# Splitting one matmul of sixteen: the frequency-0 set of a Fourier stage on TensorE

## The chip, the cores and the metric

The kernel runs on one core of a Trainium2 chip. Its time is the device time of one execution, in microseconds (us). Of the kernel before there are three runs: 596.06, 594.47 and 595.36 us, median 595.36. The profile is of one further execution, which took 595.34 us; the instructions that it records span 593.6 us.

## The reference

The output mixes two branches of the same 2048 x 512 input by a gate per row:

```python
x = A_u
g = _sigmoid((x * gate_w).sum(-1, keepdims=True))
a = _A_ref(x, ...)      # a long convolution per channel
b = _B_ref(x, ...)      # h = (x W) * (x V);  b = h W2
return g * a + (1 - g) * b

# inside _A_ref
K = 2.0 * jnp.einsum("dn,dnl->dl", C, P).real     # a filter of 2048 taps per channel
Kf = jnp.fft.rfft(K, L2)                          # L2 = 4096
Uf = jnp.fft.rfft(u_t, L2)
y = jnp.fft.irfft(Uf * Kf[None, :, :], L2)[:, :, :L]
return y + u * D_skip[None, None, :]
```

All of it is in float32.

## The kernel before

**The two branches share TensorE.** The gated product (b) is made of large matmuls, 128 rows by 128 columns with 512 columns of data, in `product` and `down`; each float32 operand there is split in a high and a low part, and three products are added (tiles `xs`, `whi`, `wlo`, `pg`, `pu`, then `hh`, `hl`, `dhi`, `dlo`, `y`). These run from the first to the last microseconds. The convolution (a) is laid between them in pieces.

**The convolution.** The filter is computed in 16 blocks of 32 channels (`k_block`, a dense run of 64 small matmuls each). After every fourth block, `transforms(q)` handles one quarter q of the channels (128 of them). A transform of length 4096 is done in two stages of small matmuls. The first stage is done ahead and its results lie in memory (`su_d` for the input, `sk_d` for the filter). For each of T = 0 to 3, `m_load` fetches the parts (512 KB each for input and filter), `m_second` does the second stage, and `m_product` multiplies input and filter spectra on VectorE. After T = 1 and T = 3, `m_inverse` and later `m_last` go back and add to the output.

**A set of the second stage.** `m_second` fills four PSUM banks. The 128 x 128 array of TensorE is used as 16 squares of 32 x 32. The row group r (32 lanes of the input tile) and the column group c pick a square, `tile_position=(32 * r, 32 * c)`; square (r, c) reads lanes 32r to 32r+31 and writes partitions 32c to 32c+31 of bank r. Each matmul has 512 columns: 256 for the filter and the input of one half p, 256 for the other half. For all frequencies but one family both halves use the same matrix, `w.t[lanes, c]`. The family with frequency 0 lies at T = 0, r = 0, c = 0, since the entries of `w2` for k = 0 stand there; it needs another matrix for the second half, which lies at index 4 of `w`. For T = 0, `w2s` thus has five matrices instead of four; in the lanes of r = 1 to 3 its fifth is equal to its first.

Before the change, all four matmuls with c = 0 of a T = 0 set are cut in two. There are four such sets, one for each q.

**Eviction.** After a set, `evict` copies each bank to the tile `ev`, on ScalarE, and for the last q every second bank on VectorE. The tiles of PSUM are called `k` in the trace.

**Order.** All operations are entered as tasks with an estimated length (1.05 us for a set), and `Work.run` lays them out by those lengths; each engine then issues in that order. An operation waits for other engines through semaphores.

Of the kernel before, what the change touches and what calls it, by code (L numbers as in the profile page):

```python
# [18 lines left out]
P = 128  # L19
# [150 lines left out]
class Work:  # L170
# [27 lines left out]
    def add(self, engine, us, fn, r=(), w=(), rank=1, after=0.0, dma=0, hold=(), rows=(), many=0):  # L198


        task = Task(len(self.tasks), engine, us, fn, rank, after, dma)
        task.rows, task.many = rows, many
        self.tasks.append(task)
        clash = lambda p, q: p is None or q is None or p == q
        split = lambda x: x if isinstance(x, tuple) else (x, None)
        for tile, part in map(split, r):
            task.deps.update(t for p, t in tile.writers if clash(p, part))
        for tile, part in map(split, w):
            task.deps.update(t for p, t in tile.writers + tile.readers if clash(p, part))
        for tile, part in map(split, r):  # L210
            tile.readers.append((part, task))
        for tile, part in map(split, w):
            tile.writers.append((part, task))
        for tile, _ in map(split, [*r, *w, *hold]):
            if tile.pool and tile not in task.tiles:
                task.tiles.append(tile)
                tile.users.append(task)
        task.deps.discard(task)
        return task
# [105 lines left out]
def gated_mix_kernel(  # L325
# [16 lines left out]
    pe, dve, act, sp, pool_q = (InOrder(tc, e) for e in (nc.tensor, nc.vector, nc.scalar, nc.sync, nc.gpsimd))  # L342
# [22 lines left out]
    def new(pool, tag, shape, dtype=F32, bufs=1, loose=False):  # L365
        return work.tile(pools[pool], tag, shape, dtype, bufs, loose)

    def bank():
        return new("ps_k", "k", [P, D], bufs=4, loose=True)
# [603 lines left out]
    def x_table(b):  # L973

        x, ri, (su, di) = xtab[b], ris[b], sus[b]
        ps = new("tab", "ps", [P, TB, 4])
        lead = [(x, ("l", k)) for k in range(3)]
        tt(0.26, lambda: ps.t, lambda: x.t[:, 0, :, 0:4], lambda: x.t[:, 1, :, 0:4], ALU.add, lead, [ps])
        outer(
            x, lambda: x.t[:, :, :, 0:4], lambda: ps.t, lambda: ri.t[:, :, :, W_M],  # L980
            lambda: su.t[:, :, W_M], lambda: di.t[:, :, 4:11], [*lead, ps, ri, su, di],
        )
        return x
# [54 lines left out]
    def apart_of(q):  # L1038
        return work.LESS if q >= KT - 2 else work.APART
# [76 lines left out]
    def evict(q, n, us, to, src, r, w):  # L1116

        if q == KT - 1 and n % 2:
            add("dve", us + 0.1, lambda: dve.tensor_copy(to(), src()), r=r, w=w)
        else:  # L1120
            add("act", us, lambda: act.copy(to(), src()), r=r, w=w)
# [35 lines left out]
    def m_second(q, T, ins, w):  # L1157

        banks = [bank() for _ in range(4)]
        to = new("mid", "ev", [P, 2, 2, 2, 2 * P], bufs=2)  # L1160
        at, parts = ins

        def fn():
            src = at().rearrange("l (p c) w d -> l c p (w d)", p=2)
            for c in range(4):
                for r in range(4):
                    lanes, to = slice(32 * r, 32 * r + 32), banks[r].t[32 * c : 32 * c + 32]
                    pieces = [(c, to, src[lanes, c])]
                    if T == 0 and c == 0:

                        pieces = [(4 * p, to[:, 2 * P * p : 2 * P * p + 2 * P], src[lanes, c, p]) for p in range(2)]
                    for m, to, x in pieces:
                        pe.matmul(to, w.t[lanes, m], x, start=True, stop=True, tile_position=(32 * r, 32 * c))

        add("pe", 1.05, fn, r=[*parts, w], w=banks, rank=1, hold=[to], many=apart_of(q))
        for r in range(4):
            h, e = divmod(r, 2)
            evict(
                q, r, 0.59, lambda h=h, e=e: to.t[:, :, e, :, P * h : P * h + P],
                lambda r=r: banks[r].t.rearrange("l (p w d) -> l w p d", p=2, w=2), [banks[r]], [(to, r)],  # L1180
            )
        return to
# [198 lines left out]
    x = x_table(0)  # L1381
    for b in range(NB):
# [5 lines left out]
        if b + 1 < NB:  # L1388
            direct_powers(b + 1)
            leads(b + 1)  # L1390
            x = x_table(b + 1)
# [59 lines left out]
```

## Time and profile before

| | |
|---|---|
| median of three runs | 595.36 us (594.47 to 596.06) |
| profiled execution | 595.34 us, span 593.6 us |
| TensorE matmul busy | 579.7 us, 98% of the span |
| VectorE busy | 512.1 us, 86% |
| ScalarE busy | 401.8 us, 68% |
| granted TensorE clock, mean | 0.996 |

PE is the matmul side of TensorE, PEld its weight loads, DVE is VectorE, ACT ScalarE, POOL GpSimd, SP SyncE. L124 is the line through which the kernel issues all its operations, so rows are told apart by their tiles: `k<-in,w2s` and `k<-x,w2s` are matmuls of the second stage when their form is `32*32` (32 rows by 32 columns). In the rows of the trace, "start us, us" come first, and `x40` counts records. A float32 matmul of this type leaves two records, one for each of its two passes.

In the table of stretches a row gives the stretch, its length, busy time with the number of records, the granted clock, the DMA share and GB/s. In the table of waits a row ends with the us in total, the times and the longest.

### The profile page before, as it was taken

The numbers are of one execution on the slowest core, as the hardware profiler recorded it, in microseconds if no ns is written. First come the engines' busy times: TensorE is split into PE (matmuls) and PEld (weight loads), VectorE is DVE, ScalarE is ACT, GpSimd is POOL, SyncE is SP. The second block draws the span as 40 slices with busy tenths as digits, with TensorE's granted clock in tenths as the row PEclk, the third lists the DMA queues.
The fourth block names the chain that finished last, engine by engine and source line by source line (L and its number), as shares of the span: only waits on it lengthen the run. The fifth ranks groups of instructions, "written<-read, shape, count | busy, mean of one in ns | idle before, by whom it ended". The sixth has DMA issues, their size and how long they took to land.

```text
span 593.6 us, 14891 instructions
## 1 busy us (share of the span) xinstructions
PE 579.7 (98%) x6020; PEld 436.6 (74%) x6020; DVE 512.1 (86%) x812; ACT 401.8 (68%) x891; POOL 113.7 (19%) x159
## 2 busy tenths in 40 slices
PE   8899999999999999899999999999999899999996
PEld 5677676788877777687676877867877776777764
DVE  6998999999998999899999999996999972556845
ACT  5348898898679488878887675799786343433351
POOL 0003212411111231310123201112422104202011
PEclk9989999999999999999999999999999999999999
DMA  8998779896867697998789856899969349898887
GB/s 270 408 368 299 273 274 347 199 309 197 204 178 204 203 239 189 227 267 263 153 200 264 188 149 190 177 279 260 225 137 251 68 131 252 271 285 207 262 187 132
DMA packets 71687, 136.28 MB, mean 230 GB/s; under 512 B 6852, under 2 KB 35780, under 8 KB 69188
## 3 DMA queue, kind: packets, MB, share of 16 engines
q1 hardware_dynamic: 47668, 87.10, 43.0%
q0 software_dynamic: 23392, 47.98, 38.6%
q8 instruction: 47, 0.77, 0.5%
q10 hardware_dynamic: 560, 0.26, 0.2%
q14 instruction: 20, 0.16, 0.1%
HBM read 80.27 MB, written 55.05 MB: 228 GB/s over the span
## 4 chain that ended last, share of the span: by engine, by line
PE 90%; DVE 5%; issue 2%; ACT 2%; DMA 1%; DVEq 0%; SPq 0%; ACTq 0%
PE pg L124 25%; PE y L124 24%; PE pu L124 24%; PE k L124 16%; DVE x L124 1%; DMA y<-in_xT 1%; DVE v L124 1%; DVE wlo L124 1%; DVE in L124 0%; ACT acc L124 0%; DMA raw<-in_xT 0%; DVE h L124 0%; DVE dlo L124 0%; ACT L124 0%; ACT xs L124 0%
## 5 line engine op out<-in xcount | busy, mean ns | idle before, releaser
L124 PE MATMUL pg<-xs,whi 128*128 128x512 f32 x448 | 139.0, 391 | 0.5 <-ACT whi L124 0.5
L124 PE MATMUL pu<-xs,whi 128*128 128x512 f32 x448 | 138.6, 391 | 0.0
L124 PEld LDWEIGHTS pg<-xs,whi 128*128 128x128 f32 x448 | 84.4, 188 | 20.9 <-ACT whi L124 2.1
L124 PEld LDWEIGHTS pu<-xs,whi 128*128 128x128 f32 x448 | 84.4, 188 | 17.0
L124 PE MATMUL y<-dhi,hl 128*128 128x512 f32 x224 | 89.7, 400 | 4.3 <-ACT acc L124 2.2
L124 PE MATMUL pg<-xs,wlo 128*128 128x512 f32 x224 | 89.8, 401 | 2.2 <-issue 1.6
L124 PE MATMUL pu<-xs,wlo 128*128 128x512 f32 x224 | 90.3, 403 | 0.0
L124 PE MATMUL y<-dlo,hh 128*128 128x512 f32 x224 | 87.7, 391 | 0.2 <-DVE dlo L124 0.2
L124 PE MATMUL y<-dhi,hh 128*128 128x512 f32 x224 | 87.5, 391 | 0.0
L124 ACT COPY ev<-k 128x512 f32<-128x512 f32 x112 | 59.4, 599 | 22.6 <-PE k L124 22.5
L124 POOL DMA_DIRECT2D out<-acc x44 | 39.4, 972 | 154.9 <-ACT acc L124 150.3
L124 ACT CAST hh<-h 128x512 fp32r<-128x512 f32 x56 | 34.9, 623 | 45.7 <-DVE h L124 45.0
L124 PEld LDWEIGHTS y<-dhi,hl 128*128 128x128 f32 x224 | 42.0, 188 | 26.8 <-issue 10.6
L124 ACT ACTIVATE acc<-y,ngate 128x512 f32<-128x512 f32 x62 | 42.2, 690 | 27.5 <-PE y L124 24.4
L124 PEld LDWEIGHTS pu<-xs,wlo 128*128 128x128 f32 x224 | 42.1, 188 | 20.9 <-issue 10.5
L124 DVE TENSOR_TENSOR h<-pu,h 128x512 f32<-128x512 f32 x56 | 38.6, 690 | 21.6 <-PE pu L124 19.9
L124 PEld LDWEIGHTS pg<-xs,wlo 128*128 128x128 f32 x224 | 42.3, 189 | 17.0 <-issue 6.2
L124 ACT COPY h<-pg 128x512 f32<-128x512 f32 x56 | 33.0, 590 | 24.6 <-PE pg L124 18.2
L124 PEld LDWEIGHTS y<-dhi,hh 128*128 128x128 f32 x224 | 42.2, 188 | 9.1
L124 PEld LDWEIGHTS y<-dlo,hh 128*128 128x128 f32 x224 | 42.1, 188 | 8.6 <-DVE dlo L124 0.5
L124 DVE TENSOR_TENSOR hl<-h,hh 128x512 fp32r<-128x512 f32 x56 | 38.4, 686 | 4.0 <-ACT hh L124 3.9
L124 POOL DMA_DIRECT2D su_d<-ev x32 | 17.9, 577 | 94.4 <-ACT ev L124 94.4
(130 smaller groups left out, 985.4 us busy)
## 6 DMA issues: line engine op xcount, KB each, us to landing
xs<-xs_d SPq DMA_DIRECT2D x36, 512.0 KB, 6.1
out<-acc POOLq DMA_DIRECT2D x44, 256.0 KB, 5.4
raw<-in_wts SPq DMA_DIRECT2D x33, 256.0 KB, 6.1
xs_d<-xs SPq DMA_DIRECT2D x16, 512.0 KB, 6.0
su_d<-ev POOLq DMA_DIRECT2D x32, 256.0 KB, 6.7
y_d<-ts SPq DMA_DIRECT2D x28, 256.0 KB, 6.0
in<-su_d POOLq DMA_DIRECT2D x12, 512.0 KB, 7.7
sk_d<-ev SPq DMA_DIRECT2D x6, 1024.0 KB, 5.7
```

The lines of the kernel that those rows point to most:

```text
L124: got = getattr(self.engine, name)(*args, **kw)
```

## The change

For T = 0 only the matmul at r = 0, c = 0 is split. Its first half is issued first in the set, its second half last, with the 15 whole matmuls between. The other sets are issued as before, by the same loop over a list of jobs.

```diff
         def fn():
             src = at().rearrange("l (p c) w d -> l c p (w d)", p=2)
-            for c in range(4):
-                for r in range(4):
-                    lanes, to = slice(32 * r, 32 * r + 32), banks[r].t[32 * c : 32 * c + 32]
-                    pieces = [(c, to, src[lanes, c])]
-                    if T == 0 and c == 0:
-
-                        pieces = [(4 * p, to[:, 2 * P * p : 2 * P * p + 2 * P], src[lanes, c, p]) for p in range(2)]
-                    for m, to, x in pieces:
-                        pe.matmul(to, w.t[lanes, m], x, start=True, stop=True, tile_position=(32 * r, 32 * c))
+            jobs = [(r, c, c, slice(0, 2)) for c in range(4) for r in range(4)]
+            if T == 0:
+
+                jobs = [(0, 0, 0, 0), *jobs[1:], (0, 0, 4, 1)]
+            for r, c, m, p in jobs:
+                lanes = slice(32 * r, 32 * r + 32)
+                to = banks[r].t[32 * c : 32 * c + 32].rearrange("l (p d) -> l p d", p=2)[:, p]
+                pe.matmul(to, w.t[lanes, m], src[lanes, c, p], start=True, stop=True, tile_position=(32 * r, 32 * c))
```

On TensorE, the T = 0 set of the last quarter reads as follows (`k` a PSUM bank, `x` the loaded parts, `w2s` the matrices; minus before, plus after):

```order
 L124 MATMUL pu<-xs,wlo 128x512
 L124 MATMUL pu<-xs,whi 128x512 x2
-L124 MATMUL k<-x,w2s 32x256 x8
-L124 MATMUL k<-x,w2s 32x512 x12
+L124 MATMUL k<-x,w2s 32x256
+L124 MATMUL k<-x,w2s 32x512 x15
+L124 MATMUL k<-x,w2s 32x256
 L124 MATMUL pu<-xs,wlo 128x512
 L124 MATMUL pu<-xs,whi 128x512 x2
```

Eight halves and 12 whole matmuls became two halves and 15; what stands around the set did not move.

On ScalarE, the copies of the first T = 0 set out of PSUM (`ev<-k`), with the semaphores that each waits for:

```order
 L124 COPY h<-pg 128x512 [waits DVE_49,PE_49]
 L124 COPY ev<-k 128x2x2x128 [waits DMAHW3_49,PE_49]
-L124 COPY ev<-k 128x2x2x128 [waits PE_49] x3
+L124 COPY ev<-k 128x2x2x128 x3
 L124 CAST hh<-h 128x512 [waits DVE_49]
 L124 ACTIVATE v<-v 128x32x16 [waits DVE_49]
```

Bank 0 is now finished by the last matmul of the set, so the first copy waits for that one, and the three others have nothing left to wait for.

## Prediction

> **What bounds the kernel now.** I read the page first: busy shares, the slices, the chain that ended last. Then I asked the trace for the sets of the second Fourier stage, for what TensorE waits for, and for the places around its two late waits.
>
> ```profile
> PE 579.7 (98%) x6020; PEld 436.6 (74%) x6020; DVE 512.1 (86%) x812; ACT 401.8 (68%) x891; POOL 113.7 (19%) x159
> PEclk9989999999999999999999999999999999999999
> PE 90%; DVE 5%; issue 2%; ACT 2%; DMA 1%; DVEq 0%; SPq 0%; ACTq 0%
> 201.00:594.00 393.00, 384.49 (x4502) 1.00 0.82 211
> 588.46 0.39 PE L124 MATMUL y<-dhi,hh 128*128 128x512 f32 x1
> ```
>
> TensorE is busy for 98% of the span and holds 90% of the chain, at the full clock. The fourth row is TensorE alone from 201 us on, where the first changed set stands: 384.49 busy of 393.00, and about 5 of the missing 8.5 us lie behind its last matmul, the fifth row. So time taken from TensorE's own work should come off the end, unless TensorE then waits. Its waits from 201 us on are two:
>
> ```profile
> PE pg L124 <- issue: 1.6, 1, 1.6
> PE y L124 <- ACT acc L124: 1.5, 1, 1.5
> ```
>
> **What a split set costs today.** A set of the second stage is 16 matmuls of 32 rows by 32 columns, one for each square of the array, 512 columns wide. For T = 0 four of them are cut in two. The trace records each matmul of this type twice (two passes), so a plain set has 32 records and a T = 0 set 40. Two neighbours, with the matmul that follows each:
>
> ```profile
> 528.23 2.14 PE L124 MATMUL k<-x,w2s 32*32 32x256 f32 x40
> 530.30 0.50 PE L124 MATMUL pu<-xs,wlo 128*128 128x512 f32 x1
> 534.63 1.14 PE L124 MATMUL k<-x,w2s 32*32 32x512 f32 x32
> 535.70 0.50 PE L124 MATMUL y<-dhi,hl 128*128 128x512 f32 x1
> ```
>
> From the first matmul of the set to the next matmul behind it: 530.30 - 528.23 = 2.07 us for T = 0, 535.70 - 534.63 = 1.07 us for a plain one. The other three T = 0 sets and the plain ones read the same in a table of stretches (busy time, records):
>
> ```profile
> 201.40:203.50 2.10, 2.05 (x40) 1.00 0.81 314
> 209.85:210.93 1.08, 1.06 (x32) 1.00 1.01 307
> 316.10:318.18 2.08, 2.06 (x40) 1.00 1.23 205
> 432.93:435.00 2.07, 2.06 (x40) 1.00 0.04 8
> ```
>
> The four split sets thus pay 1.00 us each more than a plain set of equal arithmetic. Where that goes shows in the count of records begun by a given moment, first for the split set, then for the plain one (the matmul's duration in ns, first and last start, then the shapes):
>
> ```profile
> L124 PE MATMUL k<-x,w2s x12: 398/612/612, 528.2 to 528.3; 32*32 32x512 f32 x8, 32*32 32x256 f32 x4
> L124 PE MATMUL k<-x,w2s x16: 374/505/612, 528.2 to 528.5; 32*32 32x256 f32 x8, 32*32 32x512 f32 x8
> L124 PE MATMUL k<-x,w2s x18: 374/492/612, 528.2 to 528.7; 32*32 32x256 f32 x9, 32*32 32x512 f32 x9
> L124 PE MATMUL k<-x,w2s x33: 374/585/612, 528.2 to 528.9; 32*32 32x512 f32 x17, 32*32 32x256 f32 x16
> L124 PE MATMUL k<-x,w2s x40: 374/586/612, 528.2 to 529.8; 32*32 32x512 f32 x24, 32*32 32x256 f32 x16
> L124 PE MATMUL k<-x,w2s x16: 612/612/612, 534.6 to 534.7; 32*32 32x512 f32 x16
> ```
>
> In the plain set all 16 first passes begin within 0.1 us, one per square. In the split set only 12 do: four halves (their twins sit on the same squares and must wait) and eight full matmuls. That is 16 matmuls in hand, four of them held back. The seventeenth, the first of the last four full ones, begins only by 528.7, and the last record begins at 529.8 instead of about 0.55 us into the set. So my reading is that TensorE looks some 16 matmuls ahead, and that four twins in front stop the last column group.
>
> **The change, part by part.** Removed: three matmuls in each of four sets, 12 in all (24 records of matmul and 24 weight loads). Kept: one split pair, whose halves now stand first and last.
>
> The new set: the first half and 15 full matmuls are 16, so all squares begin at once as in the plain set. The second half is the seventeenth. In the old set the seventeenth began 0.4 to 0.5 us after the start (between the second and third row above). The four half passes of a square began between 528.2 and 528.9, so a half pass takes about 0.23 us, and the second half's two passes would run from 0.45 to 0.91 us of the set. The full squares run two passes of twice that, to 0.10 + 4 x 0.23 = 1.02 us. The second half is covered, by some 0.1 us. Set: 1.07 us.
>
> The unknown is that cover. Lower bound: a plain set's 1.07. Upper bound: the second half runs alone behind all others, two half passes and the rest of the drain, 1.07 + 0.53 = 1.60 us (0.53 is half a plain set, for half the columns). I take 1.07, nearest to the plain row. Sum: 4 x (2.07 - 1.07) = 4.0 us off TensorE.
>
> The page TensorE: Matmul & The Clock Gate of the Trainium skill says, in Part 3 (packing small matmuls), that a pack lasts one matmul plus about 4 ns for each further tile. By that, a sum from the number of matmuls would be 12 x 4 ns = 0.05 us. The 1.00 us that four further halves cost here does not agree with it, since twins share a square.
>
> Evictions: the four copies out of PSUM now all wait for the last matmul, because the second half ends bank 0. Before, the first copy went ahead:
>
> ```profile
> 316.12 2.13 PE L124 MATMUL k<-in,w2s 32*32 32x256 f32 x40
> 317.60 2.05 ACT L124 COPY ev<-k 128x512 f32<-128x512 f32 x4 [1.13 <-PE k L124]
> 319.18 0.69 DVE L124 TENSOR_TENSOR h<-pu,h 128x512 f32<-128x512 f32 x1 [1.18 <-PE pu L124]
> 322.04 0.70 DVE L124 TENSOR_TENSOR hl<-h,hh 128x512 fp32r<-128x512 f32 x1
> 323.10 0.39 PE L124 MATMUL y<-dhi,hl 128*128 128x512 f32 x1
> ```
>
> The copies began 1.48 us into that set (317.60 against the start at 316.12). They will begin at 1.14 (the plain set's length with its drain) plus a few hundredths, 0.3 us earlier in absolute time but 0.7 us later against TensorE. Behind them on ScalarE stands hh, and TensorE takes hl 0.36 us after it is made (323.10 - 322.74). VectorE was idle 1.18 us before h, so it can follow by 1.0 us; its row of work then sets hl, and hh (after copies that end near 319.4) is ready before that. Cost 0; with that cover gone, up to 0.3 us in a set.
>
> **The two waits.** The first changed set lies ahead of the wait at 244 us:
>
> ```profile
> 240.15 0.62 ACT L124 CAST whi<-raw 128x512 fp32r<-128x512 f32 x1 [2.17 <-PE y L124]
> 243.38 1.25 ACT L124 ACTIVATE acc<-y,ngate 128x512 f32<-128x512 f32 x2
> 244.10 0.50 PE L124 MATMUL y<-dhi,hl 128*128 128x512 f32 x1 [1.55 <-ACT acc L124]
> ```
>
> ScalarE is idle 2.17 us, then works without a pause until acc frees the accumulator. If that chain hangs on TensorE, as the row says, it moves with it. If it hangs on the arrival of raw, the first 1.0 us is lost. I count it as passed on.
>
> The second wait names no releaser. It follows a dense run of small matmuls, and only one packet moved in code ("instruction") just then:
>
> ```profile
> 459.85 2.07 PE L124 MATMUL k<-v,x 128*32 128x64 f32 x128
> 463.50 0.40 PE L124 MATMUL pg<-xs,wlo 128*128 128x512 f32 x1 [1.59 <-issue]
> q8 instruction: 47, 0.77, 0.5%
> q8 instruction: 1, 0.02, 5.1%
> ```
>
> The last row is the stretch from 461.0 to 462.2 us. I take it for late code: 47 packets of 16 KB carry TensorE's program, and the run eats 256 records in 2 us. The change makes the program shorter by 36 matmul and load records ahead of this place, so packets end elsewhere. The stall can go (-1.59) or stay (0). The three times of before, 594.47 to 596.06, differ by just that size, so the median holds it only in part; I take -0.6.
>
> **Sum.** Profiled execution: 595.34 us (span 593.6 and 1.7 around it), 0.02 from the median 595.36. 595.36 - 4.0 - 0.6 = 590.8 us.
>
> **Rivals.** (a) The chain at 244 us hangs on raw's transfer: one set's gain is lost, 591.8. For it: the 2.17 us of idle ScalarE; against it: the named releaser. 0.14. (b) The second half runs behind everything: 1.60 a set, 4 x 0.47 = 1.9 saved, 595.36 - 1.9 - 0.6 = 592.9. Against it, the seventeenth matmul of the old set begins while others run. 0.10. (c) T = 0 is slow for another reason than its twins, and a matmul less is worth only its issue: 16 start within 0.11 us, 12 x 0.007 = 0.1 us, 595.3. Against it, the stretch of late starts lies inside the set. That counts a pack as the Trainium skill's page TensorE: Matmul & The Clock Gate does, in Part 3. 0.06. (d) Slower: shifted packets starve TensorE behind more of its dense runs, 1.59 us each. From four new stalls on it is slower by over 0.3%: 595.36 - 4.0 + 4 x 1.59 = 597.7. Against it, one stall in 47 packets so far; 0.05.
>
> **The numbers.** The forecast has 0.65. A change under 0.3% (1.8 us, 593.6 to 597.1) can't be told from none. Faster: forecast, (a) and (b), 0.89, less a little for unknown waits, 0.87; same: (c) and that little, 0.08; slower 0.05. The range goes from the stall gone wholly with some luck of run to run (595.36 - 5.6 = 589.8, less 0.6) up past (b), 589.2 to 593.2; it leaves out (c), (d) and the tails.
>
> **What would show it.** Split sets of 34 records that last 1.07 us; 15 full first passes and one half within 0.1 us of their start; TensorE's wait at 243 us no longer than 1.6; the wait after the run near 460 us shorter or elsewhere. A set longer than 1.2 us breaks the reading of the 16 in hand; a wait at 243 us of 2.5 is (a).

## The result and the profile after

The changed kernel takes 591.47 us (median of nine, 588.79 to 593.89), the kernel before beside it 596.06 us (median of nine, 594.14 to 598.65). The medians lie 4.6 us apart. The ratio is 0.9921, with a 95% interval of 0.9895 to 0.9946, which is a gain of 3.2 to 6.3 us. Forecast was 595.36 to 590.8, also 4.6 us. Medians and ratios leave out one disturbed execution, of 1457.38 us, among the ten of the kernel with both edits below.

The profiled execution of the changed kernel took 588.79 us, with a span of 587.0. Its page (busy time of the engines, the granted clock in 40 slices, the chain that ended last) still shows a kernel that TensorE bounds:

```profile
PE 575.0 (98%) x5996; PEld 434.4 (74%) x5996; DVE 511.7 (87%) x812; ACT 401.3 (68%) x891; POOL 113.8 (19%) x159
PEclk9999999999999999999999999999999999999999
PE 89%; DVE 4%; DMA 2%; ACT 2%; issue 1%; DVEq 0%; SPq 0%; ACTq 0%
```

The busy time fell by 4.7 us (579.7 to 575.0), with 24 matmul records fewer (6020 to 5996). The timeline of TensorE shows a split set and the matmul behind it:

```profile
522.85 1.14 PE L124 MATMUL k<-x,w2s 32*32 32x256 f32 x34
523.92 0.50 PE L124 MATMUL pu<-xs,wlo 128*128 128x512 f32 x1
```

523.92 - 522.85 = 1.07 us, as in a plain set, and 1.00 less than before. The other three read 1.07 too. The records of this set begun by four moments (duration in ns, first and last start, shapes):

```profile
L124 PE MATMUL k<-x,w2s x16: 398/612/612, 522.8 to 522.9; 32*32 32x512 f32 x15, 32*32 32x256 f32 x1
L124 PE MATMUL k<-x,w2s x17: 374/612/612, 522.8 to 523.1; 32*32 32x512 f32 x15, 32*32 32x256 f32 x2
L124 PE MATMUL k<-x,w2s x33: 374/588/612, 522.8 to 523.4; 32*32 32x512 f32 x30, 32*32 32x256 f32 x3
L124 PE MATMUL k<-x,w2s x34: 374/588/612, 522.8 to 523.5; 32*32 32x512 f32 x30, 32*32 32x256 f32 x4
```

Fifteen whole matmuls and one half begin within 0.1 us. The half's second pass follows alone at 0.24 us, the second half's first pass among the second passes of the others, its last pass at 0.67 us. The last whole pass begins at 0.55 us and takes twice as long as a half pass, so it ends later: the second half is covered.

The evictions behind the second split set (timeline; in brackets the idle time ahead and what ended it):

```profile
313.56 2.06 ACT L124 COPY ev<-k 128x512 f32<-128x512 f32 x4 [0.99 <-PE k L124]
317.15 0.69 DVE L124 TENSOR_TENSOR hl<-h,hh 128x512 fp32r<-128x512 f32 x1
318.19 0.39 PE L124 MATMUL y<-dhi,hl 128*128 128x512 f32 x1
```

The copies begin 1.34 us after the set (313.56 against 312.22), 1.48 before. TensorE takes hl 0.35 us after it is made, 0.36 before: nothing lost.

TensorE's late waits are of the same two kinds, those without a releaser at other places (all its waits from 199.6 us on, then the timeline):

```profile
PE y L124 <- issue: 1.6, 1, 1.6
PE y L124 <- ACT acc L124: 0.3, 1, 0.3
PE k L124 <- issue: 0.2, 1, 0.2
```

```profile
240.11 0.50 PE L124 MATMUL y<-dhi,hl 128*128 128x512 f32 x1 [0.34 <-ACT acc L124]
413.21 0.39 PE L124 MATMUL y<-dlo,hh 128*128 128x512 f32 x1 [1.57 <-issue]
```

The wait for acc is 0.34 us in place of 1.55. The wait without a releaser, 1.59 us near 462 us before, stands at 411 us with 1.57 us. The third row is a small wait of the same kind, 0.25 us at 337.7 us; it took 0.11 us before, at 342.3 us.

Where the time between the two profiled executions goes, by the starts of the same matmuls:

| Matmul | before, us | after, us | ahead by |
|---|---|---|---|
| first split set | 201.45 | 199.68 | 1.77 |
| plain set behind it | 209.87 | 207.10 | 2.77 |
| matmul behind the wait for acc | 244.10 | 240.11 | 3.99 |
| second split set | 316.12 | 312.22 | 3.90 |
| matmul soon behind it | 324.55 | 319.64 | 4.91 |
| third split set (behind the new stall at 411) | 432.94 | 430.10 | 2.84 |
| plain set behind it | 447.67 | 443.82 | 3.85 |
| plain set behind the place of the old stall | 480.61 | 475.22 | 5.39 |
| fourth split set | 528.23 | 522.85 | 5.38 |
| plain set behind it | 534.63 | 528.22 | 6.41 |
| last matmul | 588.46 | 582.05 | 6.41 |

Each split set gives 1.00 us; a row of the table can hold up to 0.03 more from what lies between its two matmuls. The first 1.77 us lie ahead of all that was changed. Some 0.6 us are lost: 0.3 at the small wait near 340 us, 0.1 near 250 us, which no row explains, and 0.2 at the moved stall, around which the matmuls lose more than its idle time.

The lead at the first set is no gain of the change. TensorE in the first 60 us (busy, records, granted clock, DMA share, GB/s), the kernel before, the changed kernel, and a second profiled execution of the changed kernel:

```profile
0.00:60.00 60.00, 55.30 (x245) 0.97 0.94 337
```

```profile
0.00:60.00 60.00, 55.97 (x257) 1.00 0.96 349
```

```profile
0.00:60.00 60.00, 55.93 (x233) 0.97 0.90 328
```

With the clock at 0.97 the changed kernel's first split set began at 202.90 us, later than before. From the first split set to the last matmul, which leaves this out, the kernel before took 387.0 us and the changed kernel 382.4 us: 4.6 us. The second profiles of the two kernels give 388.1 and 383.4 us: 4.7 us.

### The profile page after: what moved, and what is told of

Same layout as the page of the kernel before. It is cut to its first block, busy times and chain, and to the rows that moved or that the text cites. A ratio compares the mean times of both kernels' runs of the same rounds, so it can differ in the third digit from the quotient of the medians.

```text
span 587.0 us, 14842 instructions
## 1 busy us (share of the span) xinstructions
PE 575.0 (98%) x5996; PEld 434.4 (74%) x5996; DVE 511.7 (87%) x812; ACT 401.3 (68%) x891; POOL 113.8 (19%) x159
## 4 chain that ended last, share of the span: by engine, by line
PE 89%; DVE 4%; DMA 2%; ACT 2%; issue 1%; DVEq 0%; SPq 0%; ACTq 0%
PE pg L124 25%; PE pu L124 24%; PE y L124 24%; PE k L124 16%; DMA raw<-in_wts 1%; DVE x L124 1%; DVE v L124 1%; DMA y<-in_xT 1%; ACT whi L124 0%; DVE in L124 0%; DMA raw<-in_xT 0%; ACT acc L124 0%; DVE h L124 0%; DVE dlo L124 0%; ACT L124 0%
```

## The experiments

Two theories on the sets stood against each other: TensorE holds 16 matmuls of this type in hand, and what a twin in hand takes is a place; or each matmul more costs something of its own. Two more questions were the wait near 462 us and the wait for acc. The diffs are against the changed kernel.

**All twins apart.** Four split squares as before the change, with the four first halves first and the four second halves last: 20 matmuls, as before.

```diff
-                jobs = [(0, 0, 0, 0), *jobs[1:], (0, 0, 4, 1)]
+                jobs = [(r, 0, 0, 0) for r in range(4)] + jobs[4:] + [(r, 0, 4, 1) for r in range(4)]
```

> All four halves pairs of the old kernel are kept (20 matmuls in a T = 0 set), but the four first halves stand first, the 12 whole matmuls next and the four second halves last. Theory, a look-ahead of 16 matmuls that frees a place only when the oldest matmul is done: all 16 squares begin at once, the four second halves enter from 0.43 us on and the last of them begins near 0.91 us, so the set lasts about 1.2 us, and the kernel takes 4 x 0.86 = 3.4 us less than the kernel before. Rival, the cost goes by the number of matmuls: 40 records, 2.07 us a set, no gain.

592.37 us against 594.26; ratio 0.9957 (0.993 to 0.9985), a gain of 0.9 to 4.2 us where 3.4 was expected. The timeline, and the records begun within 0.1 us:

```profile
527.44 1.29 PE L124 MATMUL k<-x,w2s 32*32 32x256 f32 x40
528.67 0.50 PE L124 MATMUL pu<-xs,wlo 128*128 128x512 f32 x1
```

```profile
L124 PE MATMUL k<-x,w2s x16: 398/612/612, 527.4 to 527.5; 32*32 32x512 f32 x12, 32*32 32x256 f32 x4
```

With all 20 matmuls the set takes 1.22 us. The order alone brings 0.84 of the 1.00 us. Sixteen squares start at once, and the last record begins at 0.92 us, where 0.91 was worked out from 16 in hand. The count of matmuls is not what made T = 0 slow.

**The pair in front.** As many matmuls as in the changed kernel, but the two halves next to each other at the head.

```diff
-                jobs = [(0, 0, 0, 0), *jobs[1:], (0, 0, 4, 1)]
+                jobs = [(0, 0, 0, 0), (0, 0, 4, 1), *jobs[1:]]
```

> Only the square with frequency 0 is split, as in the changed kernel, but its two halves stand one behind the other at the front. Theory: one place of 16 is held by the twin, the last whole matmul enters when the first half's first pass is done (0.43 us), its second pass begins at 0.86 us, and the set lasts 0.86 + 0.52 = 1.37 us. Rival, the order does not matter and the number of matmuls does: 1.07 us, as in the changed kernel.

592.98 us, in a single run. The timeline, and the records begun within 0.25 us of the start:

```profile
526.73 1.44 PE L124 MATMUL k<-x,w2s 32*32 32x256 f32 x34
528.10 0.50 PE L124 MATMUL pu<-xs,wlo 128*128 128x512 f32 x1
```

```profile
L124 PE MATMUL k<-x,w2s x16: 374/612/612, 526.7 to 527.0; 32*32 32x512 f32 x14, 32*32 32x256 f32 x2
```

1.37 us, 0.30 more than the changed kernel for the same 17 matmuls. Only 14 whole ones begin at once: the second half holds a place while its square is taken, and the fifteenth comes late.

**The pair at the end.**

```diff
-                jobs = [(0, 0, 0, 0), *jobs[1:], (0, 0, 4, 1)]
+                jobs = [*jobs[1:], (0, 0, 0, 0), (0, 0, 4, 1)]
```

> Only the square with frequency 0 is split, and both halves stand at the end. Theory (a place is freed by the oldest matmul alone): the second half's first pass enters when the first whole matmul's first pass is done, at 0.64 us, its second pass when that matmul's second pass is done, at 1.07 us, and the set lasts 1.07 + 0.30 = 1.37 us. Rival, a free square is all that a matmul waits for: the second half's passes begin at 0.55 and 0.77 us, inside the run of the others, and the set lasts 1.07 us.

591.34 us, in a single run. The timeline and the records begun by three moments:

```profile
525.15 1.44 PE L124 MATMUL k<-x,w2s 32*32 32x512 f32 x34
526.52 0.50 PE L124 MATMUL pu<-xs,wlo 128*128 128x512 f32 x1
```

```profile
L124 PE MATMUL k<-x,w2s x17: 373/612/612, 525.1 to 525.5; 32*32 32x512 f32 x15, 32*32 32x256 f32 x2
L124 PE MATMUL k<-x,w2s x33: 372/588/612, 525.1 to 525.8; 32*32 32x512 f32 x30, 32*32 32x256 f32 x3
L124 PE MATMUL k<-x,w2s x34: 372/588/612, 525.1 to 526.2; 32*32 32x512 f32 x30, 32*32 32x256 f32 x4
```

1.37 us again, by another way. All 16 squares start at once here; the second half is the seventeenth. Its square is free from 0.56 us (the first half's second pass starts at 0.34 and takes 0.22), but its first pass begins at 0.64 and its second only at 1.07 us. In the trace the passes of the oldest matmul start at 0.00 and 0.45 us, so they end near 0.45 and 0.88, and each pass of the second half begins 0.19 us behind one of them. So a place comes free when the oldest matmul is done, pass by pass, not when any is.

The first of the three rows shows something more. The first half is the last of the 16 in program order, yet its second pass is the only second pass begun by 525.5 (at 0.34 us; the whole ones' begin from 0.45). Matmuls on different squares thus do not start in strict program order. The Trainium skill's page TensorE: Matmul & The Clock Gate speaks in Part 3 of a reorder window 64 deep: a float32 matmul here is two loads and two passes, and 16 x 4 = 64 agrees with all three rows of starts. Its words that matmuls start strictly in order do not agree with this row.

**No split at all.**

```diff
-                jobs = [(0, 0, 0, 0), *jobs[1:], (0, 0, 4, 1)]
+                jobs = [*jobs]
```

> No matmul of the T = 0 set is split: 16 whole ones, so that the second half of frequency 0 uses the first half's matrix (the second matrix of that frequency is left out of the computation). Theory, the second half is covered in the changed kernel: 1.07 us a set, the same time as the changed kernel, within the runs' spread. Rival, the last half still costs something (each T = 0 set shorter than 1.07, or the kernel faster by more than 0.5 us beyond the changed one's gain of about 4.6 us): the cover was not whole.

589.17 us against 594.26; ratio 0.9894 (0.9831 to 0.9956), not to be told from the changed kernel's. The kernel leaves out the second matrix of frequency 0. The timeline:

```profile
524.46 1.14 PE L124 MATMUL k<-x,w2s 32*32 32x512 f32 x32
525.53 0.50 PE L124 MATMUL pu<-xs,wlo 128*128 128x512 f32 x1
```

1.07 us, as in the changed kernel: the second half, first and last as the change has it, adds nothing to the set. The medians alone can't decide, since 5.1 us against the changed kernel's 4.6 lies at the rival's mark of 0.5 us. In the traces this kernel is 1.8 us shorter from the first T = 0 set to the last matmul (380.6 against 382.4 us), and nearly all of that stands at the wait for acc and at the waits without a releaser.

**Another order in the filter blocks.** The filter blocks are the other dense runs of small matmuls; two that follow each other there share the same columns of the array. Here neighbours stand on different columns (the arguments of the matmul, which stay, are left out of the diff).

```diff
-            for d in range(TB):
-                ch, g = d % 4, d // 4
+            for g in range(TB // 4):
                 for c in range(2):
-                    pe.matmul(
+                    for ch in range(4):
+                        d = 4 * g + ch
+                        pe.matmul(
```

> The changed kernel, and in each of the 16 filter blocks the 64 small matmuls are put in another order: the two that add up on the same strip of the array are no longer neighbours, four strips take turns (all first parts of a group of four, then all second parts). Theory, a neighbour on the same strip only costs where it fills the look-ahead of 16 and starves another strip; here 16 in hand always hold all four strips, so a block stays at 2.00 us and the kernel at the changed kernel's time within the runs' spread. Rival, neighbours on one strip always cost: 128 records at the rate of four free strips, up to 0.27 us less a block and 4 us less in all.

591.65 us; ratio 0.9934 (0.9908 to 0.9959). One block in this kernel, then in the changed kernel:

```profile
458.90 1.99 PE L124 MATMUL k<-v,x 128*32 128x64 f32 x128
460.83 0.50 PE L124 MATMUL pg<-xs,wlo 128*128 128x512 f32 x1
```

```profile
456.00 2.07 PE L124 MATMUL k<-v,x 128*32 128x64 f32 x128
457.99 0.50 PE L124 MATMUL pg<-xs,wlo 128*128 128x512 f32 x1
```

460.83 - 458.90 = 1.93 against 1.99 us. With the matmul ahead a block takes 2.24 against 2.31 us, 16 x 0.07 = 1.1 us over the kernel. Neither expectation was met: the theory had no change in a block, the rival up to 0.27 us. So 16 matmuls in hand do not explain all that neighbours on one strip cost; what the 0.07 us are was not found. The total does not show them.

**What the wait near 462 us is.** The trace was counted up to the place of the stall: all of TensorE's records, its matmuls and loads and the few others it kept (86 before, 76 after). These rows are stretches of all engines up to the stall; the two first counts are TensorE's matmuls and its loads. Before, then after:

```profile
0.00:461.90 461.90, 454.44 (x4661) 344.96 (x4662) 432.42 (x687) 352.66 (x792) 92.84 (x138) 1.00 0.85 238
```

```profile
0.00:412.00 412.00, 405.92 (x4154) 307.81 (x4155) 389.07 (x623) 320.22 (x717) 79.59 (x126) 1.00 0.85 245
```

4661 + 4662 + 86 = 9409 and 4154 + 4155 + 76 = 8385. They differ by 1024 = 4 x 256, a whole number of packets of 16 KB if a packet holds 256 records. (The kernel before has 12155 such records and 47 packets of code, 259 to a packet.) If the stall is code that comes late, the length of the program ahead must move it. Nine tiny matmuls at the start of the kernel are 36 records and put back what three changed sets took away (3 x 3 matmuls); 32 are another shift:

```diff
             for _ in range(2):
                 pe.matmul(scratch.t, zero.t[:, :P], zero.t, start=True, stop=True)
+            for _ in range(9):
+                pe.matmul(scratch.t[:32, :8], zero.t[:, :32], zero.t[:, :8], start=True, stop=True)
```

> The changed kernel with nine tiny matmuls (32 rows and columns wide, 8 columns of data) added behind the two at the very start, 36 more records for TensorE's program to fetch. In the profiles so far TensorE's wait without a releaser came when 9409 records had begun (before) and when 8385 had begun (changed kernel), which is the same place in a packet of 256. Theory, late code: the places where packets end lie in the program as in the kernel before from the third changed set on, so the wait of about 1.6 us comes behind the filter block near 458 us again, at record 9409; wherever one comes, it is at 193 modulo 256. Rival, the wait belongs to that work or to the moment: it stays at 411 us, at record 8421.

> As the run with nine tiny matmuls, with 32 of them, 128 records or half a packet. Theory, late code: the packets end half a packet away from the places of the changed kernel, so no wait without a releaser at its place near 411 us (record 8513 here); any that there is stands at 193 modulo 256. Rival: the wait near 411 us stays, at record 8513.

594.9 us with nine, 590.25 us with 32, a single run each. A stall in the timeline of each:

```profile
464.22 0.50 PE L124 MATMUL pg<-xs,whi 128*128 128x512 f32 x1 [1.92 <-issue]
```

```profile
149.73 0.50 PE L124 MATMUL pu<-xs,wlo 128*128 128x512 f32 x1 [0.80 <-issue]
```

With nine it is back where it stood before, again at record 9409, and none is left at 411 us; three more stand at records 1729 (1.00 us), 4801 (2.33) and 6593 (1.01). The view puts the one at 4801 down to ScalarE's v; its place in the count is that of the others. With 32 the one at 411 us is gone, and one of 0.80 us stands at record 2241. All these counts leave 193 when divided by 256. So these are stalls at the end of a stretch of 256 records, and padding that changes no other work moves them.

The small wait near 340 us is one of them too. It stands at record 6593 in all ten profiles without the 32 matmuls, from 0.11 to 1.01 us long. In the kernel before, profiled again:

```profile
342.97 0.48 PE L124 MATMUL k<-y,w3s 32*64 32x128 f32 x16 [0.72 <-issue]
```

The packets of code in the traces settle what is late. In the kernel before a packet is moved from 461.10 to 462.08 us, and TensorE goes on at 463.50; in the changed kernel one is moved from 410.78 to 411.76 us, and TensorE goes on at 413.21. In all twelve profiles 24 such stalls of 0.1 us or more stand, and each ends 1.2 to 1.5 us after such a packet, though these come some 12 us apart: late code.

**Both together.** The other order of the filter blocks with the 32 tiny matmuls, which between them should have taken away block time and stall:

> The changed kernel with the two edits that looked best together: the filter blocks in the order of four strips in turn (each block 2.24 instead of 2.31 us from the matmul ahead to the matmul behind, 16 x 0.07 = 1.1 us) and 32 tiny matmuls at the start, which shift the ends of the code packets by half a packet. Theory: 1.1 us from the blocks for certain, and the wait at record 8385 gone (1.0 to 1.6 us), unless another packet ends late: about 589.5 where the changed kernel has 591.5, any wait without a releaser at 193 modulo 256. Rival: the waits for code only change places, and the gain is 1.1 us or less.

590.65 us; ratio 0.9925 (0.989 to 0.9961), no better than the changed kernel's 0.9921, where 2 us more were expected. The blocks take 2.24 us, as expected, and one stall of 1.08 us at record 2241 is left, against 1.82 and 1.43 us of stalls in the changed kernel's two profiles. But the 32 matmuls have a price that the expectation put at nothing: behind the wait for acc near 89 us TensorE goes on at 89.39 us (89.31 with the 32 matmuls alone), against 88.44 in the changed kernel, all with the clock at 1.00.

**The same kernels again.** Nothing edited; the changed kernel and the kernel before, each profiled once more, for what one execution differs from the next.

> The changed kernel once more, unaltered, for a second profile. Theory: sets with T = 0 at 1.07 us; the wait without a releaser again at record 8385, since the packets of code are the same, between 1.0 and 2.0 us; the wait for acc near 240 us anywhere from 0 to 2 us, since it follows how long the transfer of raw takes (5.8 to 9.9 us so far). Rival, that wait is settled by TensorE's progress: 0.4 us as in the first profile.

> The kernel before once more, unaltered, for a second profile. Theory: T = 0 sets at 2.07 us; the wait without a releaser at record 9409 again, 1.0 to 1.7 us; the wait for acc near 242 us anywhere from 0 to 2 us, by how long the transfer of raw takes. Rival: the wait near 461 us was chance and does not come again, so that the change has not moved it.

593.01 and 596.14 us, a single run each. The wait for acc and the cast ahead of it, the changed kernel again, then the kernel before again:

```profile
240.74 0.62 ACT L124 CAST whi<-raw 128x512 fp32r<-128x512 f32 x1 [2.33 <-DMA raw<-in_wts]
244.70 0.53 PE L124 MATMUL y<-dhi,hl 128*128 128x512 f32 x1 [1.66 <-ACT acc L124]
```

```profile
240.22 0.62 ACT L124 CAST whi<-raw 128x512 fp32r<-128x512 f32 x1 [2.40 <-DMA raw<-in_wts]
244.17 0.50 PE L124 MATMUL y<-dhi,hl 128*128 128x512 f32 x1 [1.66 <-ACT acc L124]
```

The same changed kernel waits 0.34 us for acc in one execution and 1.66 in the next, and the releaser is now the transfer of raw in both kernels, also in the one whose first profile named TensorE's y. There too the cast began at 240.15 us, when the raw issued at 231.62 us had landed, 8.45 us later, at 240.07. The two transfers of raw issued ahead of this place landed after (min, median, max) in the kernel before, the changed kernel, the changed kernel again and the unsplit one:

```profile
DMA to landing us min/median/max: 8.3/8.4/8.5
```

```profile
DMA to landing us min/median/max: 6.2/7.3/8.5
```

```profile
DMA to landing us min/median/max: 9.2/9.4/9.5
```

```profile
DMA to landing us min/median/max: 5.8/6.7/7.7
```

Where the first landing took 6.2 us or less, the wait for acc is 0 to 0.34 us; where it took 8.3 or more, 1.5 to 1.7 us, in all twelve profiles. The chain hangs on raw. The stall came at the same records as in the first profiles, 8385 (1.02 us) and 9409 (1.55 us), with the small one at 6593 in both (0.41 and 0.72 us).

## Why the prediction was right

**The split sets: right, to a hundredth.** 4 x 1.00 us was the main term, and each set gave it: 1.07 us, 34 records, 15 whole matmuls and a half within 0.1 us. The reading of 16 in hand held in four orders: 1.07, 1.22, 1.37 and 1.37 us, the last three expected at about 1.2, 1.37 and 1.37 before they ran. The upper bound of 1.60 (rival b) did not occur; with the pair at the end, the nearest case to it, a set takes 1.37. Rival (c), a cost per matmul, falls with the twins apart: 20 matmuls take 1.22 us, not 2.07. What the prediction left out is how a place comes free; it was not needed for this order, in which the oldest matmul is itself a half and done early.

**The cover and the evictions: right.** The unsplit set takes the same 1.07 us, so the second half is free. The copies began 1.34 us into the set, not near 1.2, and the slack ahead of hl stayed: cost 0.

**The wait at 244 us: the number right, the mechanism wrong.** The prediction let the chain hang on TensorE and its gain pass on. The chain hangs on raw, as rival (a) had it. But (a)'s loss of 1.0 us did not follow. Raw's issue itself came earlier behind the shorter set: 30.2 and 29.1 us after the first split set's start in the two profiles before, 28.3 and 28.2 us in the two after. And the transfer, 6 or 9 us long, spreads the wait by more than the change moves it. Between the two first profiles the wait gave 1.21 us, which was luck; between the two second ones it gave nothing (1.66 us in both).

**The wait near 462 us: the step that failed.** It was rightly taken for late code, but the term of -0.6 us rests on a stall that goes or stays, and it did neither: the shorter program moved it from 462 to 411 us. That packets "end elsewhere" was seen; that the stall comes at the next place was not counted. In idle time the move gave 0.02 us between the first profiles (1.59 to 1.57) and 0.53 between the second ones (1.55 to 1.02). Over all profiles with a stall there, the place at 9409 costs 1.5 to 1.9 us and the one at 8385 1.0 to 1.6, or 0.66 without any split. Nor was the spread of the first three runs the stall's coming and going: it stands in both profiles of the kernel before.

**The total: part of the match is luck.** Without this term the sum is 595.36 - 4.0 = 591.4 us, next to a measured 591.47. But beside the changed kernel the kernel before took 596.06 us, and from there the sets alone give 592.1. The gain of 4.6 us is known only to within 3.2 to 6.3; the 4.0 us are shown by the sets, not by the total.

**The rival with many stalls.** Rival (d) did not occur in the changed kernel. But the kernel with nine tiny matmuls shows four stalls, 6.3 us in all against the changed kernel's 1.8, and at 594.9 us lies near the kernel before.

**What stays open.** What sets the length of a stall is not known: the one at record 6593 took 0.11 and 0.72 us in the same kernel. Why a transfer of raw takes 6 us in one execution and 9 in another was not found.

## What to carry to other kernels

In sets of small matmuls on squares of the array, count what TensorE holds in hand (here 16 float32 matmuls) and put two that share a square as far apart as the set allows, one first and one last: the cover was complete. When a stall sits at a fixed count of instructions, any edit that shortens or lengthens the program ahead of it can move it, so no gain is to be booked for it, and a change of a few us is to be judged over several executions, with the profile saying which waits are the change's. Take the named releaser of a wait for several things with care, and look at a second profile before resting a term on it.

## What the runs showed of the hardware

Stalls of 0.1 to 2.3 us came at records of TensorE that leave 193 on division by 256: 8385 in the changed kernel and 9409 in the kernel before, both times each was profiled, 6593 in both, and 1729, 2241 and 4801 in others. Each ends 1.2 to 1.5 us after a packet of code has been moved. Whether one occurs at such a place differs: 47 or 48 packets of code are moved in a run and one to four stalls show.

The same transfer of 256 KB took 5.6 to 9.8 us from issue to landing in kernels whose work around it is the same. And the clock granted in the first 60 us was 0.97 in eight profiles and 1.00 in four. At 0.97 the first T = 0 set began at 201.2 to 203.1 us; at 1.00, in the two kernels without added matmuls, at 199.6 and 199.7.
